# An attention and gated feed-forward kernel on one core: the second unit's softmax sums inverted on GpSimd, the third unit's outputs as three accumulating products, and an earlier copy of transposed scores

## The chip, the cores and the metric

The kernel runs on one core of one Trainium2 chip. A core has five engines that run their own instruction streams in order and meet through semaphores: TensorE (PE in the profile; its weight loads are listed as PEld), VectorE (DVE), ScalarE (ACT), GpSimd (POOL) and SyncE (SP), which here issues the DMAs. The metric is the device time of one execution in microseconds. Before the change it is 1147.95 us, the median of three runs (1147.83 to 1148.65).

## The reference

The reference has two parts. First comes masked attention over q, k, v of 8 batches, 8 heads, 576 positions and 64 values a head. The first four heads see the last 32 positions, the last four every fourth of the last 128:

```python
scores = scale * np.matmul(q, k.transpose(0, 1, 3, 2))
mask_plain = (rel >= 0) & (rel < window)
mask_dil = (rel >= 0) & (rel < window * dilation) & (rel % dilation == 0)
scores = np.where(masks[None, :, :, :], scores, -1000000000.0)
attn = np.exp(scores - np.max(scores, axis=-1, keepdims=True))
attn = attn / (np.sum(attn, axis=-1, keepdims=True) + 1e-09)
return np.matmul(attn, v)
```

The heads are put side by side, which makes x with 4608 rows of 512, and x goes through a normalised, gated feed-forward layer of width 1536:

```python
xn = x / np.sqrt(np.mean(x * x, axis=-1, keepdims=True) + 1e-06) * rms_g
g = xn @ w_gate
silu = g * (1.0 / (1.0 + np.exp(-g)))
return silu * (xn @ w_val) @ w_out
```

All values are float32. The weights arrive as 64-bit floating-point words and are turned into 32-bit ones on the chip.

## The kernel before

**Units and bursts.** The 4608 rows are cut into 16 units of 288 (half a batch each). The attention of a unit is cut into 14 bursts: a pair of heads with 96 queries (three bursts for each of the first two pairs) or 72 queries (four for each of the last two). A burst goes through these stages: the scores on TensorE (`scored`, L486 or L489), their maximum on DVE (`scores_max`, L361 and L366), the exponentials on ACT, which also add up the sums (`scores_exp`, L376), the inversion of the sum and the scaling by it (`scores_norm`, L384 to L393), the transposition on TensorE (`transposed`, L463), its copy out of PSUM (`untranspose`, L446 and L448), the product with v (`output`, L472, or L477 and L478), and the copy of the outputs into x (`take`, L408 or L411, and for some units `add`, L421).

**Exact and split units.** The first two units (`u < NNAT`, NNAT is 2) multiply plain float32 numbers. From the third on, every operand is split into a rounded high part and a low part in float32r, and a product is made of three: high by high, high by low, low by high. For the outputs of these units the kernel makes one wide product of v's high part with both parts of the scores (L477: 4 times the queries as columns) and one of v's low part (L478: 2 times), the latter added in PSUM to the first half of the former. The two halves are then added in SBUF: `take` copies the second half (ACT, L411), `add` adds the first half from PSUM (DVE, L421).

**The scaling of a burst.** For the first unit it stands on DVE mostly, for the second on ACT (L389), from the third on, on POOL (L391). The sum and its inverse are made on DVE for all of them (L385 and L386; before that, in the first unit, L384).

**The feed-forward layer.** A unit's layer is 12 rounds of three program steps: `gate` (the gate's products of one block of 128 columns; part 0), `val` (the value's products; part 1), and `proj` (the output products of the block before; part 2). The gate's and the value's products go to two PSUM banks in turn: the gate of the next block takes the bank of this block's value. A bank is free when the value product on DVE (`prod`, L679) has read it and, where a transposition was written into the rest of the same bank, when that has been copied out too. Outputs of attention have one bank, scores one.

**Order.** Nothing is reordered: the program's order is each engine's order. One number, `now`, counts the program steps; `later(dt, rank, fn)` puts work off to the start of a later step, and `flush` emits it there by rank, ahead of the products of that step. A burst's scores are made in some step; the maximum follows one step later, the exponentials two (rank 2), for the second unit the inversion and the scaling three (rank 2.1). Transpositions follow after 5 steps, the second unit's outputs after 7 and the third unit's after 8. The attention of a unit lies beside the feed-forward layer of the unit before it.

**What else lies beside the second unit's attention.** While the first unit's layer runs (about 41 to 129 us), the weights are still being decoded. A piece is loaded by DMA, rebased (`rebase`: ACT L159 makes a scaled copy, then POOL L162 scales the piece in place), and put together by two operations on DVE in two successive steps (`rest`, L177, and `whole`, L181). The rebasing of the next piece is emitted at the end of the step in which `rest` was emitted (rank 8.9). In every second step a weight is also split for the later units (rank 6: ACT L242 and then DVE or POOL L243).

**Other lines named below.** `gate` puts a tanh on ACT (L661) and a product on DVE (L666); `square` (ACT L427, then L433 on POOL or DVE) sums the squares for the normalisation; `rms_root` (L536 to L543) takes the root on POOL; `split_v` makes the parts of v (ACT L301, POOL L305); `split` those of q and k (L330 to L344); `parts` those of the hidden values (ACT L690, POOL L691).

Of the kernel before, what the change touches and what calls it, by code (L numbers as in the profile page):

```python
# [9 lines left out]
F32 = mybir.dt.float32  # L10
# [4 lines left out]
ALU = mybir.AluOpType  # L15
# [10 lines left out]
QB = 96  # L26
NC = DM // P
NJ = FF // P
NNAT = 2
# [23 lines left out]
def geometry(u, c):  # L53


    half = u % 2
    if c < NC // 2:
        if half:
            return [(QB * i, QB * i, 0, P) for i in range(U // QB)], QB, U + W
        return [(QB * i, max(QB * i - W, 0), 0 if i else W, P if i else QB)  # L60
                for i in range(U // QB)], QB, U
    nq = U // DIL
    keys = nq + (W if half else 0)
    return [(nq * r, keys * r, 0 if half else W, keys) for r in range(DIL)], nq, keys * DIL
# [3 lines left out]
def attn_moe(ctx: ExitStack, tc: tile.TileContext, qk_in, v_in, w_gate, w_val, w_out, rms_g, outT):  # L68
# [4 lines left out]
    V, A, G, PE = nc.vector, nc.scalar, nc.gpsimd, nc.tensor  # L73

    cst = ctx.enter_context(tc.tile_pool(name="cst", bufs=1))
# [11 lines left out]
    G.memset(inv, 1.0 / DM)  # L87
    mhalf = cst.tile([QB, U // QB], F32, name="mhalf")
    G.memset(mhalf, -0.5)
    mask = cst.tile([QB, P], F32, name="mask")  # L90
    G.memset(mask, 0.0)
    G.affine_select(out=mask, in_=mask, pattern=[[-1, P]], compare_op=ALU.is_ge,
# [14 lines left out]
    now = [0]  # L107
    put_off = {}

    def later(dt, rank, fn):  # L110
        put_off.setdefault(now[0] + dt, []).append((rank, fn))
# [173 lines left out]
    def further(b, n):  # L285

        k = everything.index(b) + n
        return everything[k] if k < len(everything) else None
# [90 lines left out]
    def scores_norm(u, c, i):  # L379
        blocks, nq, _ = geometry(u, c)  # L380
        n = blocks[i][3]
        t, sm = st[u, c, i]
        if u == 0:
            V.tensor_reduce(out=sm[:nq, :, 1], in_=t[:nq, :, :n], axis=mybir.AxisListType.X, op=ALU.add)  # L384
        V.tensor_reduce(out=sm[:nq, :, 3], in_=sm[:nq, :, 1:3], axis=mybir.AxisListType.X, op=ALU.add)  # L385
        V.reciprocal(out=sm[:nq, :, 3], in_=sm[:nq, :, 3])  # L386
        for a in range(2):
            if u == 1:
                A.activation(out=t[:nq, a, :n], in_=t[:nq, a, :n], func=AF.Copy, scale=sm[:nq, a, 3:4])  # L389
                continue  # L390
            (V if u == 0 and (c, i) > (NC - 1, 0) else G).tensor_scalar(  # L391
                out=t[:nq, a, :n], in0=t[:nq, a, :n], scalar1=sm[:nq, a, 3:4],
                scalar2=1.0, op0=ALU.mult, op1=ALU.mult)  # L393

    def take(u, c, i, o):

        blocks, nq, _ = geometry(u, c)
        if (u, c) not in xraw:
            xraw[u, c] = sb.tile([P, U], F32, tag="xraw", name=f"xraw_{u}_{c}", bufs=NC)
        x = xraw[u, c]  # L400
        if c < NC // 2:
            to = x[:, QB * i:QB * i + nq]
        else:
            to = x.rearrange("p (j r) -> p r j", r=DIL)[:, i, :]
        copy = V.tensor_copy if i % 2 and u == 0 and c == NC - 1 else A.copy
        if u < NNAT:
            for a in range(2):
                copy(out=to[a * D:(a + 1) * D], in_=o[a * D:(a + 1) * D, a * nq:(a + 1) * nq])  # L408
        else:
            for a in range(2):  # L410
                A.copy(out=to[a * D:(a + 1) * D], in_=o[a * D:(a + 1) * D, (2 + a) * nq:(3 + a) * nq])  # L411
        if i == len(blocks) - 1:
            later(1, 2.5 if u else 1.9, lambda: square(u, c))
# [9 lines left out]
    def square(u, c):  # L423
        first = c == 0
        sq = sb.tile([P, U], F32, tag="xsq" if first else "tmp", name=f"sq_{u}_{c}", bufs=1 if first else 2)
        x = xraw[u, c]
        A.activation(out=sq, in_=x, func=AF.Square)  # L427
        if u == 0:
            G.tensor_scalar(out=x, in0=x, scalar1=gs[:, c:c + 1], scalar2=1.0, op0=ALU.mult, op1=ALU.mult)
        if first:  # L430
            xsq[u] = sq
        else:
            later(1, 0.4, lambda: (V if c == NC - 1 else G).tensor_tensor(out=xsq[u], in0=xsq[u], in1=sq, op=ALU.add))  # L433
# [6 lines left out]
    def untranspose(b, t_ps):  # L440
        blocks, nq, _ = geometry(*b[:2])
        n = blocks[b[2]][3]
        t_in = t_ps[:n].rearrange("k (a q) -> k a q", a=2)[:, :, :nq]
        exact = b[0] < NNAT
        st[b] = pt = sb.tile([P, 2, 2, QB], F32 if exact else F32R, tag="pt", name=f"pt_{b[0]}_{b[1]}_{b[2]}", bufs=2)
        A.copy(out=pt[:n, 0, :, :nq], in_=t_in)  # L446
        if not exact:
            V.tensor_tensor(out=pt[:n, 1, :, :nq], in0=t_in, in1=pt[:n, 0, :, :nq], op=ALU.subtract)  # L448

    def products(q, t, o, t_ps, s_tag="s", o_tag="o"):  # L450


        if q:
            s_ps = ps.tile([P, 512], F32, tag=s_tag, name=f"s_{q[0]}_{q[1]}_{q[2]}")
        if o:
            o_ps = ps.tile([P, 512], F32, tag=o_tag, name=f"o_{o[0]}_{o[1]}_{o[2]}")
            pt = st.pop(o)
        if t:
            p, _ = st.pop(t)
        def transposed(a):  # L460
            blocks, nq, _ = geometry(*t[:2])
            n = blocks[t[2]][3]
            PE.transpose(t_ps[:n, a * QB:a * QB + nq], p[:nq, a, :n], ident[:nq, :nq])  # L463

        def output(a):
            blocks, nq, _ = geometry(*o[:2])
            n = blocks[o[2]][3]
            if a:
                return
            out = o_ps[:, :2 * nq].rearrange("d (a q) -> d a q", a=2)  # L470
            if o[0] < NNAT:
                PE.matmul(out, vs.pop(o)[:n].rearrange("k a d -> k (a d)"), pt[:n, 0, :, :nq], start=True, stop=True)  # L472
                return
            vh, vl = (part[:n].rearrange("k a d -> k (a d)") for part in vparts[everything.index(o) % 2])

            both = o_ps[:, :4 * nq].rearrange("d (t a q) -> d t a q", t=2, a=2)
            PE.matmul(both, vh, pt[:n, :, :, :nq], start=True, stop=False)  # L477
            PE.matmul(out, vl, pt[:n, 0, :, :nq], start=False, stop=True)  # L478

        def scored(a):  # L480
            blocks, nq, _ = geometry(*q[:2])
            qc, kc, _, n = blocks[q[2]]
            sv = s_ps[:QB].rearrange("q (a t k) -> q a t k", a=2, t=2)
            if q[0] < NNAT:
                qk = heads[q[0], 2 * q[1] + a]
                PE.matmul(sv[:nq, a, 0, :n], qk[:, qc:qc + nq], qk[:, U + kc:U + kc + n], start=True, stop=True)  # L486
                return
            qs, ks = heads[q[0], 2 * q[1] + a]
            PE.matmul(sv[:nq, a, :, :n], qs[:, qc:qc + nq], ks[:, :, kc:kc + n], start=True, stop=True)  # L489

        parts = [(b, fn, a) for b, fn in ((t, transposed), (o, output), (q, scored)) for a in range(2)]
        for b, fn, a in parts:
            if b:
                fn(a)
        if t:
            later(1, 0.2, lambda: untranspose(t, t_ps))
        if o:
            later(1, 0.5, lambda: take(*o, o_ps))
            if o[0] >= NNAT:
                later(1, 4, lambda: add(*o, o_ps))  # L500
            if o[0] < NNAT:
                later(1, 9, lambda: load_v(further(o, 3)))
            far = further(o, 2)
            if far and far[0] >= NNAT:
                split_v(far, 11 if o[0] < NNAT else 1)
        if q:
            later(1, 0.7, lambda: scores_max(*q, s_ps))
            later(2, 2, lambda: scores_exp(*q))
            later(3 if q[0] < NNAT else 4, 2.1 if q[0] == 1 else -1, lambda: scores_norm(*q))
            u, c, i = q  # L510
            nxt = after(u, 2 * c, 2)
            nb = len(geometry(u, c)[0])
            if u < NNAT:
                if u == NNAT - 1 and c == NC - 1 and i == nb - 1:
                    for a in range(2):
                        later(1, 9, lambda a=a: load(NNAT, a))
                        later(5 + a, 9, lambda a=a: split(NNAT, a, (1, 2, 2, 3), G, V))
            elif nxt and i == 0:
                split(*nxt, (1, 2, 2, 3), G, V)
                split(nxt[0], nxt[1] + 1, (2, 3, 3, 4), G, V)  # L520
# [240 lines left out]
    ends = nb + LAG + OUT + 5  # L761
# [8 lines left out]
    for n in range(ends):  # L770
# [4 lines left out]
        t_ps = None  # L775
        if "t" in events.get(n, {}):
            t_ps = ps.tile([P, 512], F32, tag="gv"[n % 2] if n < nb + LAG else "acc0", name=f"t_first_{n}")[:, :2 * QB]
# [12 lines left out]
    for u in range(NU):  # L790
        for j in range(NJ):
            for part in range(0 if u + j else 2, 3):
                t = 3 * (u * NJ + j) + part
# [92 lines left out]
```

## Time and profile before

| what | value |
|---|---|
| median of three runs | 1147.95 us (1147.83 to 1148.65) |
| the profiled execution | 1148.22 us |
| its span | 1146.4 us |
| granted TensorE clock, mean | 0.997 |
| PE, busy | 1120.8 us (98%) |
| DVE, busy | 793.4 us (69%) |
| ACT, busy | 714.6 us (62%) |
| POOL, busy | 620.8 us (54%) |
| chain that ended last | PE 85%, DVE 6%, ACT 4%, issue 2%, DMA 1%, POOL 1% |

A row of the timeline gives the start and the time taken in us, the engine, the line of the kernel, the operation, what is written and read, and its shape; in brackets stands how long the engine had been idle before it, and what ended that. A row of the waits gives the engine and line that waited, the one it waited for, the us in total, how often, and the longest. The busy time of TensorE is no measure of its full speed, since successive products overlap; a gap between them is lost time all the same.

### The profile page before, as it was taken

What the parts mean: (1) busy time and instruction counts of PE and PEld (TensorE: products, weight loads), DVE (VectorE), ACT (ScalarE), POOL (GpSimd) and SP (SyncE); (2) the same over time, 40 slices, a digit from 0 to 9 for tenths busy, and PEclk for the clock granted to TensorE, in tenths of its full rate; (3) what the DMA queues carried; (4) which work ended last, traced back from release to release, by engine and by line L of the source; (5) the groups of instructions that cost most, each with busy time, mean ns of one, the idle gap of its engine ahead of it and who ended that gap; (6) DMA issues with size and microseconds to landing.
All of it is one profiled execution on the core that took longest, in us unless ns stands there. A gap on an engine that the chain in (4) does not pass through costs nothing.

```text
span 1146.4 us, 25956 instructions
## 1 busy us (share of the span) xinstructions
PE 1120.8 (98%) x8357; PEld 1088.0 (95%) x8357; DVE 793.4 (69%) x2893; ACT 714.6 (62%) x2610; POOL 620.8 (54%) x1073
## 2 busy tenths in 40 slices
PE   8898888999999999999999999999999999999998
PEld 7676778999999999999999999999999999999998
DVE  7889865867767586776758677585866758586411
ACT  5686676766657576675757657576765757576311
POOL 8235576655546465564547556465655646565211
PEclk9999999999999999999999999999999999999999
DMA  9555211311212121121212213121221312120000
GB/s 246 168 202 205 89 48 38 93 50 50 83 38 82 40 84 52 52 89 33 79 41 83 58 41 94 34 86 41 71 63 45 95 27 87 41 79 15 2 21 21
DMA packets 61545, 82.19 MB, mean 72 GB/s; under 512 B 7298, under 2 KB 41090, under 8 KB 61410
## 3 DMA queue, kind: packets, MB, share of 16 engines
q1 hardware_dynamic: 61410, 80.54, 23.6%
q8 instruction: 67, 1.10, 0.4%
q14 instruction: 68, 0.56, 0.2%
HBM read 71.08 MB, written 9.44 MB: 70 GB/s over the span
## 4 chain that ended last, share of the span: by engine, by line
PE 85%; DVE 6%; ACT 4%; issue 2%; DMA 1%; POOL 1%; POOLq 0%; SPq 0%; DVEq 0%; ACTq 0%
PE acc L622 8%; PE g L622 8%; PE v L622 8%; PE acc L623 8%; PE g L624 8%; PE g L623 8%; PE acc L624 8%; PE v L623 8%; PE v L624 8%; PE s L489 3%; PE o L477 3%; PE o L478 1%; PE busy L739 1%; ACT t L376 1%; DVE lo L243 1%
## 5 line engine op out<-in xcount | busy, mean ns | idle before, releaser
L691 POOL TENSOR_TENSOR hlo<-th,hhi 128x288 fp32r<-128x288 f32 x180 | 145.2, 807 | 201.5 <-ACT hhi L690 153.7
L624 PE MATMUL acc<-hhi,lo 128*128 128x288 f32 x720 | 212.2, 295 | 0.0
L391 POOL TENSOR_SCALAR t<-t,sum 72x72 f32<-72x72 f32 (+3 forms) x414 | 154.0, 384 | 71.9 <-DVE sum L386 65.2
L624 PE MATMUL v<-xhi,lo 128*128 128x288 f32 x612 | 180.8, 295 | 0.0
L624 PE MATMUL g<-xhi,lo 128*128 128x288 f32 x612 | 180.6, 295 | 0.0
L376 ACT ACTIVATE t<-t,sum 96x128 f32<-96x128 f32 (+3 forms) x448 | 165.6, 375 | 11.7 <-DVE sum L366 11.0
L690 ACT CAST hhi<-th 128x288 fp32r<-128x288 f32 x180 | 78.1, 434 | 141.0 <-DVE th L679 138.8
L305 POOL TENSOR_TENSOR vlo<-vt,vhi 128x128 fp32r<-128x128 f32 x196 | 93.3, 476 | 109.3 <-ACT vhi L301 96.9
L421 DVE TENSOR_TENSOR xraw<-o,xraw 64x96 f32<-64x96 f32 (+1 forms) x392 | 106.8, 272 | 56.4 <-ACT xraw L411 50.4
L661 ACT ACTIVATE th<-g 128x288 f32<-128x288 f32 x180 | 73.9, 410 | 106.6 <-PE g L624 87.7
L624 PEld LDWEIGHTS acc<-hhi,lo 128*128 128x128 f32 x720 | 135.6, 188 | 0.0
L666 DVE SCALAR_TENSOR_TENSOR th<-th,g 128x288 f32<-128x288 f32 x180 | 80.4, 447 | 69.4 <-ACT th L661 69.4
L624 PEld LDWEIGHTS v<-xhi,lo 128*128 128x128 f32 x612 | 115.3, 188 | 0.0
L624 PEld LDWEIGHTS g<-xhi,lo 128*128 128x128 f32 x612 | 115.0, 188 | 0.0
L622 PE MATMUL g<-xhi,hi_g 128*128 128x288 f32 x357 | 110.7, 310 | 1.6 <-DVE sum L385 0.9
L335 POOL TENSOR_TENSOR ks<-qk,ks 128x288 fp32r<-128x288 f32 (+2 forms) x112 | 111.0, 1005 | 0.0
L622 PE MATMUL acc<-hhi,hi_o 128*128 128x288 f32 x360 | 110.8, 308 | 0.0
L411 ACT COPY xraw<-o 64x96 f32<-64x96 f32 (+1 forms) x392 | 101.5, 259 | 12.5 <-PE o L478 10.1
L679 DVE TENSOR_TENSOR th<-th,v 128x288 f32<-128x288 f32 x180 | 81.5, 453 | 38.1 <-PE v L624 30.0
L623 PE MATMUL acc<-hlo,hi_o 128*128 128x288 f32 x360 | 106.9, 297 | 0.0
L361 DVE TENSOR_TENSOR t<-s,mask 96x256 f32<-96x256 f32 (+3 forms) x196 | 71.5, 365 | 50.9 <-PE s L489 45.7
L623 PE MATMUL g<-xlo,hi_g 128*128 128x288 f32 x322 | 94.8, 294 | 0.0
(184 smaller groups left out, 3581.2 us busy)
## 6 DMA issues: line engine op xcount, KB each, us to landing
qk<-in_qk_dram SPq DMA_DIRECT2D x60, 288.0 KB, 2.8
vt<-in_v_dram SPq DMA_DIRECT2D x196, 64.0 KB, 1.9
qk<-in_qk_dram SPq DMA_DIRECT2D x30, 352.0 KB, 3.0
out_dram<-ot SPq DMA_DIRECT2D x64, 144.0 KB, 1.9
qk<-in_qk_dram SPq DMA_DIRECT2D x30, 304.0 KB, 2.8
raw<-in_w_gate_dram SPq DMA_DIRECT2D x12, 512.0 KB, 4.7
raw<-in_w_val_dram SPq DMA_DIRECT2D x12, 512.0 KB, 5.3
raw<-in_w_out_dram SPq DMA_DIRECT2D x12, 512.0 KB, 4.3
```

Source lines behind the costliest of these rows:

```text
L305: G.tensor_tensor(out=vl, in0=vs.pop(b), in1=vh, op=ALU.subtract)
L335: ek.tensor_tensor(out=ks[:, 1, :nkt], in0=kr, in1=ks[:, 0, :nkt], op=ALU.subtract)
L376: A.activation(out=t[:nq, a, :n], in_=t[:nq, a, :n], func=AF.Exp, scale=-1.0, bias=sm[:nq, a, 0:1], accum_out=sm[:nq, a, 1:2] if u else None)
L391: (V if u == 0 and (c, i) > (NC - 1, 0) else G).tensor_scalar(out=t[:nq, a, :n], in0=t[:nq, a, :n], scalar1=sm[:nq, a, 3:4], scalar2=1.0, ...
L411: A.copy(out=to[a * D:(a + 1) * D], in_=o[a * D:(a + 1) * D, (2 + a) * nq:(3 + a) * nq])
L421: V.tensor_tensor(out=to[rows], in0=o[rows, a * nq:(a + 1) * nq], in1=to[rows], op=ALU.add)
L622: PE.matmul(out, wh[:, cc, :], xh, start=start, stop=False)
L623: PE.matmul(out, wh[:, cc, :], xl, start=False, stop=False)
L624: PE.matmul(out, wl[:, cc, :], xh, start=False, stop=stop)
L666: V.scalar_tensor_tensor(out=t, in0=t, scalar=1.0, in1=g, op0=ALU.add, op1=ALU.mult)
L679: V.tensor_tensor(out=t, in0=t, in1=v_ps[:, :U], op=ALU.mult)
L691: G.tensor_tensor(out=lo, in0=t, in1=hi, op=ALU.subtract)
```

## The change

It has three parts. In the second unit (u = 1), the sum and its inverse are made on POOL, with an addition and a power of -1, in place of a reduction and a reciprocal on DVE; a small tile of -1 is set at the start. In the third unit (u = 2), the outputs are three products that accumulate in the same PSUM columns; `take` copies that half directly, and the later `add` falls away; the units after it stay as they were. And where a transposition was written into a value's bank (part 1 of a round), its copy is emitted ahead of the value product (rank -0.1 in place of 0.2; the value product has rank 0).

```diff
@@ -87,6 +87,8 @@
     mhalf = cst.tile([QB, U // QB], F32, name="mhalf")
     G.memset(mhalf, -0.5)
+    minus = cst.tile([QB, 2], F32, name="minus")
+    G.memset(minus, -1.0)
@@ -382,8 +384,12 @@
         t, sm = st[u, c, i]
         if u == 0:
             V.tensor_reduce(out=sm[:nq, :, 1], in_=t[:nq, :, :n], axis=mybir.AxisListType.X, op=ALU.add)
-        V.tensor_reduce(out=sm[:nq, :, 3], in_=sm[:nq, :, 1:3], axis=mybir.AxisListType.X, op=ALU.add)
-        V.reciprocal(out=sm[:nq, :, 3], in_=sm[:nq, :, 3])
+        if u == 1:
+            G.tensor_tensor(out=sm[:nq, :, 3], in0=sm[:nq, :, 1], in1=sm[:nq, :, 2], op=ALU.add)
+            G.tensor_tensor(out=sm[:nq, :, 3], in0=sm[:nq, :, 3], in1=minus[:nq], op=ALU.pow)
+        else:
+            V.tensor_reduce(out=sm[:nq, :, 3], in_=sm[:nq, :, 1:3], axis=mybir.AxisListType.X, op=ALU.add)
+            V.reciprocal(out=sm[:nq, :, 3], in_=sm[:nq, :, 3])
@@ -403,7 +409,7 @@
-        if u < NNAT:
+        if u <= NNAT:
             for a in range(2):
                 copy(out=to[a * D:(a + 1) * D], in_=o[a * D:(a + 1) * D, a * nq:(a + 1) * nq])
         else:
@@ -472,6 +478,10 @@
             vh, vl = (part[:n].rearrange("k a d -> k (a d)") for part in vparts[everything.index(o) % 2])
+            if o[0] == NNAT:
+                for k, (vp, t) in enumerate(((vh, 0), (vh, 1), (vl, 0))):
+                    PE.matmul(out, vp, pt[:n, t, :, :nq], start=k == 0, stop=k == 2)
+                return
@@ -493,10 +503,10 @@
         if t:
-            later(1, 0.2, lambda: untranspose(t, t_ps))
+            later(1, -0.1 if now[0] >= ends and (now[0] - ends) % 3 == 2 else 0.2, lambda: untranspose(t, t_ps))
         if o:
             later(1, 0.5, lambda: take(*o, o_ps))
-            if o[0] >= NNAT:
+            if o[0] > NNAT:
                 later(1, 4, lambda: add(*o, o_ps))
```

## The prediction

> **What bounds the kernel now.** First the busy times by stretch (TensorE alone, then one stretch with all engines; the columns are the length, then busy us and count per engine), because the share over the whole span mixes stages.
>
> ```profile
> 44.00:92.00 48.00, 44.06 (x219) 0.96 0.58 209
> 200.00:1146.00 946.00, 942.18 (x7329) 1.00 0.19 57
> 60.00:80.00 20.00, 20.00 (x108) 16.30 (x107) 16.75 (x44) 18.15 (x58) 7.83 (x6) 1.00 0.55 195
> ```
>
> From 200 us on TensorE stands still for 946 - 942.18 = 3.8 us in all, and the change leaves the number of columns that it streams there as it is: nothing is to be won there. What the change can move lies before 200 us. Between 60 and 80 us TensorE is full, but ACT is at 18.15 of 20 and DVE at 16.75: ACT has almost no air, and it runs in order, so a new wait on ACT stays on ACT. POOL is at 7.83 and looks free; what matters is what stands ahead in its queue, not its load.
>
> Next, who held TensorE up between 130 and 200 us, where the third unit's attention runs:
>
> ```profile
> PE v L622 <- DVE pt L448: 3.3, 2, 1.8
> PE s L489 <- DVE sum L366: 1.7, 2, 1.0
> PE o L477 <- DVE xraw L421: 1.6, 2, 0.9
> ```
>
> DVE is the last to end in all three: here taking work off DVE pays, and at most some 10 us (these and five smaller rows of that answer).
>
> **Part 1: the second unit's inversion on POOL.** What goes is small: a sum and a reciprocal on DVE for each of 14 bursts.
>
> ```profile
> 59.49 0.15 DVE L385 TENSOR_REDUCE sum<-sum 72x2 f32<-72x4 f32 x1
> 59.67 0.16 DVE L386 RECIPROCAL sum<-sum 72x2 f32<-72x2 f32 x1
> 59.76 1.20 DVE L181 SCALAR_TENSOR_TENSOR f<-f,raw 128x1024 uint32<-128x1024 uint32 x1
> ```
>
> 14 x 0.31 = 4.3 us of DVE. What comes is an add and a power on POOL. The trace has no such pair on two columns; the nearest are the root's operations on three columns, free and beside DVE's decoding:
>
> ```profile
> 198.70 0.86 POOL L537 TENSOR_TENSOR rst<-rst,mhalf 96x3 f32<-96x3 f32 x1 [3.70 <-DVE rst L536]
> 199.89 0.46 POOL L543 TENSOR_TENSOR rst_lo<-rst,rst_hi 96x3 fp32r<-96x3 f32 x1
> 111.71 1.85 POOL L537 TENSOR_TENSOR rst<-rst,mhalf 96x3 f32<-96x3 f32 x1
> ```
>
> So the pair takes 0.46 + 0.86 and a hand-over, 1.4 us, and 2.4 us where the power is held up as at 111.71. I take 1.4 to 2.0, nearer the free rows, since two columns are less than three. The Trainium skill (SBUF — State Buffer, section Who interferes with whom) says that a DVE instruction with two SBUF inputs and a GpSimd one share a port pair, and that whichever starts first holds it for its whole length. The rows of L537 (0.86 and 1.85) agree; by that rule each of the pair could wait out a 1.2 us decoding operation, an estimate of up to 3.8 us for both, and part 1 would come out at its high end below, 10.5.
>
> The price is not the pair but its place. The inversion's result is waited for by ACT's scaling (L389) in the same step. In every second step a weight piece was rebased at the step's end: ACT L159, then POOL L162, which waits for L159. The inversion of the following step stands behind that L162. Five of the fourteen bursts fall so. DVE could do its two operations at once; POOL can't.
>
> *Place 1, at 60 us.* ACT, then POOL, from narrow windows of the timeline (start, us, and in brackets the idle time before):
>
> ```profile
> 58.63 1.14 ACT L159 ACTIVATE f<-raw 128x1024 f32<-128x1024 f32 x1
> 59.79 0.32 ACT L446 COPY pt<-v 128x192 f32<-128x192 f32 x1
> 60.01 0.65 ACT L389 ACTIVATE t<-t,sum 72x104 f32<-72x104 f32 x2
> 61.41 0.47 ACT L408 COPY xraw<-o 64x96 f32<-64x96 f32 x2
> 62.66 1.16 ACT L159 ACTIVATE f<-raw 128x1024 f32<-128x1024 f32 x1
> 65.64 0.64 ACT L389 ACTIVATE t<-t,sum 72x104 f32<-72x104 f32 x2
> 59.85 2.12 POOL L162 TENSOR_SCALAR raw<-raw 128x1024 f32<-128x1024 f32 x1 [4.12 <-DVE sum L386]
> 63.96 1.12 POOL L162 TENSOR_SCALAR raw<-raw 128x1024 f32<-128x1024 f32 x1 [2.00 <-ACT f L159]
> ```
>
> L162 starts at 59.85 and takes 1.12 when free, 2.12 beside DVE's L181: it ends between 61.0 and 62.0. With the pair, L389 starts between 62.4 and 64.0 instead of 60.01; I take 63.1, so ACT is 3.1 late. Behind L389 stand the squares, the weight split, and the copies of the last outputs (L408, ended 61.88). There is one bank for outputs, so TensorE's next outputs wait for these copies. TensorE's places, here and below:
>
> ```profile
> 63.68 0.52 PE L472 MATMUL o<-pt,v 128*128 128x192 f32 x2
> 68.74 0.34 PE L486 MATMUL s<-qk 128*72 128x104 f32 x2
> 78.57 0.46 PE L472 MATMUL o<-pt,v 104*128 104x144 f32 x2
> 84.17 0.51 PE L619 MATMUL g<-xn,f 128*128 128x288 f32 x1 [0.50 <-ACT pt L446]
> ```
>
> 61.88 + 3.1 = 65.0 against 63.68: TensorE 1.3 late (0.5 to 2.2).
>
> *Place 2, at 65.64.* ACT carries its 3.1 along. L159 now ends at 63.82 + 3.1 = 66.9, L162 at 68.05, the pair at 69.5 to 70.1; I take 70.0. ACT itself would be there at 65.64 + 3.1 = 68.7, so 1.3 comes on top: 4.4 late. Behind L389 come the weight split's copy, DVE's half of the split, the value product and the scores' maximum, which frees the one bank of scores:
>
> ```profile
> 68.16 0.08 DVE L366 DVE_READ_ACCUMULATOR2_ANT sum<- 72x1 f32 x1
> ```
>
> It ended at 68.24, TensorE's scores came at 68.74: 0.5 of air, TensorE 3.9 late (2.4 to 4.6).
>
> *Places 3 and 4, at 76 and 82.*
>
> ```profile
> 74.76 1.15 ACT L159 ACTIVATE f<-raw 128x1024 f32<-128x1024 f32 x1
> 76.11 0.65 ACT L389 ACTIVATE t<-t,sum 72x104 f32<-72x104 f32 x2
> 77.18 0.58 ACT L408 COPY xraw<-o 64x72 f32<-64x72 f32 x2
> 78.53 1.19 ACT L159 ACTIVATE f<-raw 128x1024 f32<-128x1024 f32 x1
> 81.57 0.64 ACT L389 ACTIVATE t<-t,sum 72x104 f32<-72x104 f32 x2
> 77.66 1.22 POOL L433 TENSOR_TENSOR sq<-sq,sq 128x288 f32<-128x288 f32 x1
> ```
>
> ACT has some air in between and comes to place 3 about 3.1 late, paced by TensorE (3.9 less 0.8, the air at 78.57 counted below). L159 ends at 75.91 + 3.1 = 79.0, L162 at 80.15; the sum of squares (L433) stands ahead of the inversion too: 81.4; the pair ends at 82.8 to 83.4, I take 83.1. ACT is 7.0 late. The copies that ended at 77.76 end at 84.8 and the outputs of 78.57 wait: TensorE 6.2 late. Place 4: L159 ends at 79.72 + 7.0 = 86.7, L162 at 87.85, the pair at 89.3 to 89.9, I take 89.8; ACT alone would come at 88.6: 1.2 more, 8.2 late. That reaches the gate products of 84.17 through the split and the value product. They also waited 0.50 for the copy at that place, which part 3 puts ahead: some 0.35 comes back, TensorE 7.9 late. The two steps after give back about 0.5 (waits of that size on ACT, which is then less late than TensorE). A fifth place, near 49 us, costs 0 to 1.3, since ACT comes there early; I take 0.3. The sum is 7.9 - 0.5 + 0.3 = 7.7, with 4.5 at every low end and 10.5 at every high end. From 92 to 130 us DVE's decoding runs in the same order behind the same late steps; I see nothing in it that makes the time good.
>
> **Part 2: the third unit's outputs.** 28 additions leave DVE:
>
> ```profile
> 130.00:200.00 70.00, 7.61 (x28) 0.98 0.19 54
> ```
>
> That is DVE's time at L421 alone. It counts only where DVE ends a wait: the output bank is free after ACT's copies (the 1.6 us above go), and two additions, 0.54, come out of the chain ahead of four waits of scores and gates. Not all of it stays, for ACT's chain (output copies, exponentials, splits) is next late at three of these places. I take 2.5 in all together with part 3, between 0.5 (the bank alone, and another wait taking most of it) and 6.0 (over half of the 10 us).
>
> On TensorE, one product of 288 columns and one of 144 become three of 144:
>
> ```profile
> 178.67 0.37 PE L477 MATMUL o<-pt,vhi 72*128 72x288 f32 x1 [0.91 <-DVE xraw L421]
> 178.88 0.23 PE L478 MATMUL o<-pt,vlo 72*128 72x144 f32 x1
> 178.95 0.34 PE L622 MATMUL v<-xhi,hi_o 128*128 128x288 f32 x1
> ```
>
> From start to start 0.21 and 0.07, 0.28 in all; three of 0.07 are 0.21. The number of columns is the same, so I take 0 for the 14 bursts, with -1.0 (14 x 0.07) and +0.7 as the ends, since one more weight load could show. The Trainium skill (TensorE: Matmul & The Clock Gate, section Back-to-back issue gap) gives about 81 ns for 128 columns; with that, an estimate, three would take 0.24 and the sum would move by less than 0.6 over all bursts.
>
> **Part 3: the copy first in a value's bank.**
>
> ```profile
> ACT pt L446 <- DVE th L679: 101.2, 70, 2.5
> ```
>
> ACT's copy waited 70 times for the value product, which reads the same bank; the order is now turned round, and the product waits for the copy. Where DVE is last, ACT's copy and the hand-over, some 0.4 us, leave the chain to the next gate products (in part 2's 2.5). Where ACT is last, DVE stands behind it: at 59.79 the copy came right after L159, and the product, with DVE's decoding behind it, now waits for it. That costs nothing extra while ACT holds DVE at L243 anyway. From 200 us on there is room in both orders; I take 0, up to +1.
>
> **The sum.** The profiled execution took 1148.22 us (span 1146.4); 1148.22 + 7.7 - 2.5 = 1153.4. It lies 0.3 above the median of the runs, 1147.95; so 1153.1. Ends: +4.5 - 6.0 = -1.5 gives 1146.5; +10.5 - 0.5 + 1 = 11 gives 1159.0.
>
> **Rivals.**
> *POOL is in time.* If POOL ran the inversion ahead (the exponentials' sums are there a step earlier), ACT would lose nothing and even save its waits for the reciprocal, and parts 2 and 3 would remain: 1148 - 2.5 - 0.5 = 1145. For it: nine of fourteen inversions have a free POOL ahead of them. Against it: the five rows of L162 and L389; an in-order queue can't pass L162. It decides at the air of 1.8 us at 63.68. 0.15.
> *It cancels.* The low end of part 1 against the high end of part 2: 1147 to 1149. 0.10.
> *The shared port makes it worse.* Each of the pair is held up by DVE's decoding in all bursts, by 1 us or more: part 1 reaches 10 or over, 1157 to 1160. For it: 111.71. Against it: at the five places DVE mostly waits for ACT just then. 0.12.
> *The product behind the copy becomes a bound* after 200 us, where ACT is inside another operation: TensorE's 3.8 us of standing still would double, with part 1 as forecast 1157. 0.05.
> My forecast: 0.58.
>
> **Chances.** About 0.2%, 2.3 us, is what a measurement can tell from no change. Slower by more: 0.58 + 0.12 + 0.05 = 0.75; within: 0.10; faster: 0.15. The range 1146.5 to 1159.0 leaves out most of the first rival and the upper part of the third, under 0.2.
>
> **What would show it.** Right: ACT waits for POOL at L389 near 60, 66, 76 and 82 us, 8 us or more in all; outputs on TensorE wait for L408 near 64 and 80; 92 us of before comes near 99. L421 is gone, TensorE's waits between the third unit's bursts shrink by 2 to 3 us. Wrong: L389 starting without a wait, or TensorE as full between 55 and 83 us as before; or the third unit's stretch shorter by 5 us or more.

## The result and the profile after

The changed kernel takes 1162.51 us, the median of four runs (1161.36 to 1162.87), against 1147.89 us for the kernel before beside it: a ratio of 1.0126 [1.0108, 1.0143]. It is slower by 14.6 us, on the side that the prediction took and 9.4 us beyond its value, outside its range. The profiled execution took 1162.32 us, its span is 1160.2 us.

In the new file lines have moved: the rebasing is L161 and L164, the inversion L388 and L389, ACT's scaling L395, the output copies L414 and L417, the additions L427, the copies of transposed scores L452 and L454, the second unit's outputs L478, the value product L689, the rounding of the hidden values L700.

TensorE by stretch (length, busy us and count, clock, DMA share, GB/s):

```profile
44.00:92.00 48.00, 39.00 (x180) 0.89 0.43 152
92.00:130.00 38.00, 33.72 (x144) 0.96 0.58 202
130.00:200.00 70.00, 61.12 (x414) 0.98 0.19 57
200.00:1160.00 960.00, 952.95 (x7407) 1.00 0.19 56
```

Between 44 and 92 us TensorE issues 180 products in place of 219, stands still for 9.0 us in place of 3.9, and its granted clock has gone from 0.96 to 0.89. After 200 us it stands still for 7.05 us in place of 3.8. Following one and the same product through both traces gives the delay directly: 10.8 us at 130 us, some 9.9 at 200, 13.8 at the end. So the loss has three parts: +10.8 where the second unit's attention lies, -0.9 where the third's lies, and +3.9 over the rest.

**The first stretch.** ACT's largest row of waits between 30 and 105 us, and the five scalings that waited longest (in brackets the idle time and what ended it):

```profile
ACT t L395 <- POOL sum L389: 12.9, 7, 3.6
```

```profile
49.80 0.69 ACT L395 ACTIVATE t<-t,sum 96x128 f32<-96x128 f32 x2 [2.27 <-POOL sum L389]
64.58 0.65 ACT L395 ACTIVATE t<-t,sum 72x104 f32<-72x104 f32 x2 [2.85 <-POOL sum L389]
71.55 0.38 ACT L395 ACTIVATE t<-t,sum 72x104 f32<-72x104 f32 x1 [1.28 <-POOL sum L389]
86.19 0.65 ACT L395 ACTIVATE t<-t,sum 72x104 f32<-72x104 f32 x2 [3.62 <-POOL sum L389]
92.92 0.38 ACT L395 ACTIVATE t<-t,sum 72x104 f32<-72x104 f32 x1 [1.21 <-POOL sum L389]
```

What stood ahead of the second and the fourth in POOL's queue:

```profile
61.47 1.14 POOL L164 TENSOR_SCALAR raw<-raw 128x1024 f32<-128x1024 f32 x1 [4.61 <-ACT f L161]
62.55 1.21 POOL L388 TENSOR_TENSOR sum<-sum 72x2 f32<-72x2 f32 x1
63.85 0.70 POOL L389 TENSOR_TENSOR sum<-sum,minus 72x2 f32<-72x2 f32 x1
...
82.36 1.13 POOL L164 TENSOR_SCALAR raw<-raw 128x1024 f32<-128x1024 f32 x1 [3.83 <-ACT f L161]
83.43 1.79 POOL L439 TENSOR_TENSOR sq<-sq,sq 128x288 f32<-128x288 f32 x1
85.18 0.19 POOL L388 TENSOR_TENSOR sum<-sum 72x2 f32<-72x2 f32 x1
85.45 0.70 POOL L389 TENSOR_TENSOR sum<-sum,minus 72x2 f32<-72x2 f32 x1
```

POOL stood idle for 4.61 and 3.83 us ahead of L164, which waited for ACT; then came L164, once the sum of squares, and only then the pair. These are the five places and the order that the prediction named. From its start to its end the pair takes 1.0 us where nothing holds it up, as at 85.18, and 2.0 where the addition is held up, as at 62.55.

TensorE's standstills that followed, and its clock in three windows of the length in which that changes:

```profile
52.56 0.97 PE L496 MATMUL s<-qk 128*72 128x104 f32 x4 [3.98 <-DVE sum L368]
74.22 0.40 PE L496 MATMUL s<-qk 128*72 128x104 f32 x2 [2.41 <-DVE sum L368]
87.87 0.51 PE L478 MATMUL o<-pt,v 104*128 104x144 f32 x2 [1.73 <-ACT xraw L414]
95.23 0.51 PE L629 MATMUL g<-xn,f 128*128 128x288 f32 x1 [2.20 <-DVE h L689]
```

```profile
51.40:58.23 6.83, 5.67 (x17) 0.50 0.44 149
75.30:78.71 3.41, 3.41 (x12) 0.50 0.20 49
95.80:99.21 3.41, 3.41 (x10) 0.50 0.57 205
```

The clock is exactly halved, for 3.41 us or twice that. The first stretch begins within the standstill of 3.98 us, the other two 1.1 and 0.5 us behind those of 2.41 and 2.20 us; a fourth comes at 181.1 us. The kernel before has one such stretch in these places and one later:

```profile
52.30:55.71 3.41, 3.41 (x10) 0.50 0.48 196
147.90:151.31 3.41, 3.41 (x18) 0.50 0.02 5
```

Up to 130 us, half of TensorE's busy time at half clock is lost: (5.67 + 3.41 + 3.41) / 2 = 6.2 us after, 3.41 / 2 = 1.7 before, so, as an estimate, up to 4.5 us of the 10.8 is clock and not waiting. The Trainium skill (TensorE: Matmul & The Clock Gate, section What's actually happening) tells of a free-running window of 3413 ns and a gate that passes either all pulses or half of them, with half after an idle window; the stretches agree in length and in depth, but the standstill of 2.20 us ahead of 95.8 us is shorter than such a window.

**The later stretches.** Who held TensorE up between 130 and 205 us, the rows that answer to those of before:

```profile
PE v L632 <- DVE pt L454: 3.3, 3, 1.6
PE g L629 <- DVE h L689: 1.1, 1, 1.1
```

The wait of the outputs for the additions (1.6 us) is gone; that of the scores for the maxima (1.7) is down to 0.2. From 205 us on these rows lead; the kernel before has the second with 0.4 us and nothing like the first:

```profile
PE o L487 <- DVE xraw L427: 2.2, 6, 0.4
PE o L487 <- ACT pt L452: 1.0, 1, 1.0
```

### The profile page after: what moved, and what is told of

It reads as the page before. It is cut to its first block, busy times and chain, and to the rows that moved or that the text cites. A ratio compares the mean times of both kernels' runs of the same rounds, so it can differ in the third digit from the quotient of the medians.

```text
span 1160.2 us, 25893 instructions
## 1 busy us (share of the span) xinstructions
PE 1127.4 (97%) x8371; PEld 1092.4 (94%) x8371; DVE 783.1 (67%) x2837; ACT 720.8 (62%) x2610; POOL 640.2 (55%) x1102
## 4 chain that ended last, share of the span: by engine, by line
PE 81%; DVE 6%; ACT 6%; POOL 3%; issue 2%; DMA 1%; POOLq 0%; SPq 0%; DVEq 0%; ACTq 0%
PE acc L632 8%; PE v L632 8%; PE g L632 8%; PE acc L633 7%; PE v L633 7%; PE v L634 7%; PE g L634 7%; PE g L633 7%; PE acc L634 7%; PE s L499 3%; PE o L487 2%; PE busy L749 1%; DVE qs L346 1%; PE o L488 1%; PE g L629 1%
## 5 line engine op out<-in xcount | busy, mean ns | idle before, releaser
L700 ACT CAST hhi<-th 128x288 fp32r<-128x288 f32 x180 | 77.9, 433 | 202.3 <-DVE th L689 197.7
L427 DVE TENSOR_TENSOR xraw<-o,xraw 64x72 f32<-64x72 f32 (+1 forms) x364 | 99.2, 273 | 53.0 <-ACT xraw L417 48.4
L689 DVE TENSOR_TENSOR th<-th,v 128x288 f32<-128x288 f32 x180 | 81.0, 450 | 32.3 <-PE v L634 31.0
L346 DVE TENSOR_TENSOR qs<-qk,qs 64x288 fp32r<-64x288 f32 x112 | 91.3, 816 | 11.0 <-ACT qs L341 7.9
L417 ACT COPY xraw<-o 64x72 f32<-64x72 f32 (+1 forms) x364 | 93.8, 258 | 7.2 <-PE o L488 5.1
```

Source lines behind the costliest of these rows:

```text
L346: eq.tensor_tensor(out=qs[D:], in0=qr[D:], in1=qs[D:], op=ALU.subtract)
L427: V.tensor_tensor(out=to[rows], in0=o[rows, a * nq:(a + 1) * nq], in1=to[rows], op=ALU.add)
L689: V.tensor_tensor(out=t, in0=t, in1=v_ps[:, :U], op=ALU.mult)
```

## The experiments

The medians, with the kernel before in the same comparison. The first four kernels ran on one chip, the next four on a second and the last three on a third, so kernels of different groups are compared by their ratios.

| kernel | what it has | median us | before us | ratio |
|---|---|---|---|---|
| p1_only | part 1 | 1158.68 | 1148.71 | 1.0086 [1.0069, 1.0103] |
| p2_only | part 2 | 1146.25 | 1148.71 | 0.9973 [0.9962, 0.9984] |
| p3_only | part 3 | 1154.99 | 1148.71 | 1.0055 [1.0040, 1.0070] |
| p1_nine | part 1 for nine bursts | 1145.40 | 1148.71 | 0.9973 [0.9962, 0.9985] |
| p1_early | part 1, issued a step earlier | 1145.56 | 1148.26 | 0.9976 [0.9966, 0.9986] |
| p1_fill | part 1, TensorE kept busy | 1154.63 | 1148.26 | 1.0052 [1.0037, 1.0067] |
| p3_skip | part 3 without three copies | 1149.60 | 1148.26 | 1.0014 [1.0004, 1.0024] |
| nine_p2 | p1_nine and part 2 | 1143.03 | 1148.26 | 0.9951 [0.9936, 0.9966] |
| before_fill | before, TensorE kept busy | 1148.25 | 1148.67 | 0.9997 [0.9988, 1.0007] |
| p2_p3 | parts 2 and 3 | 1152.25 | 1148.67 | 1.0033 [1.0024, 1.0043] |
| early_p2 | p1_early and part 2 | 1143.18 | 1148.67 | 0.9948 [0.9934, 0.9963] |

**Each part alone.** Each kernel takes its part's lines of the change's diff and no others.

Part 1:

> The inversion on GpSimd alone. If the place in GpSimd's queue is what costs (five inversions behind a rebase): TensorE stands still about 6 to 7 us more than before between 44 and 100 us, with the half-speed stretches that follow about 10 us in all, so 1156 to 1160. If the loss of the full change came from its parts together (the value product behind the copy): under 1153.

Part 2:

> The three products without the later additions, alone. My forecast said about 2 us faster: 1145.5 to 1147. The rival, that another wait takes the place of the removed one: within 0.5 us of before.

Part 3:

> The copy first, alone. If it is this part that costs some 0.35 us in every second unit after 200 us (the outputs wait for the later addition): 2 to 4 us slower from 200 us on, 1149.5 to 1152 in all. If the 4 us lost there in the full change were late transfers by chance: 1147 to 1149.

Part 1 costs 10.0 us, part 2 brings 2.5, part 3 costs 6.3, which is above both of its expected ranges: they had left out that it costs early as well. The sum, 13.8, is within a microsecond of the whole change's 14.6, but in part by chance. By stretch the parts don't add: at 130 us the delays of parts 1 and 3, 10.2 and 3.0, would make 13.2 where the changed kernel is 10.8 late, and between 130 and 200 us it wins 0.9 where part 2 alone wins 2.0. Part 1's delay stands at 10.2 us at 130 us and moves little afterwards (10.85 at the end). Part 2's gain falls where it was looked for, 2.0 us of it between 130 and 200 us. The kernel before has a halved stretch at 147.9 us and part 2 alone has none there, but that isn't the gain: p1_only and before_fill have none there either, and against the kernel before they stand at 200 us where they stood at 140, within 0.1 us. Part 3's cost, which the prediction put at 0 to 1, has two halves: 3.0 us up to 130 us and 3.5 after 200.

**Is it the place in POOL's queue, or the pair itself?** Two kernels change the place and leave the pair's operations as they are. In p1_nine the five bursts whose scaling waited behind a rebasing keep their inversion on DVE:

```diff
-        if u == 1:
+        if u == 1 and now[0] - ends + 2 not in (4, 8, 10, 14, 16):
             G.tensor_tensor(out=sm[:nq, :, 3], in0=sm[:nq, :, 1], in1=sm[:nq, :, 2], op=ALU.add)
```

> The inversion on GpSimd alone, but the five bursts whose inversion stands behind a rebase keep it on VectorE. By place: nothing is lost, 1147 to 1149. By the price of the operations on GpSimd: nine fourteenths of the loss of the first kernel, about 6 us, so 1153 to 1155.

In p1_early all fourteen are on POOL, issued at the end of `scores_exp`, one step earlier and so ahead of the rebasing:

```diff
     def scores_exp(u, c, i):
...
+        if u == 1:
+            G.tensor_tensor(out=sm[:nq, :, 3], in0=sm[:nq, :, 1], in1=sm[:nq, :, 2], op=ALU.add)
+            G.tensor_tensor(out=sm[:nq, :, 3], in0=sm[:nq, :, 3], in1=minus[:nq], op=ALU.pow)
...
     def scores_norm(u, c, i):
...
-        if u == 1:
-            G.tensor_tensor(out=sm[:nq, :, 3], in0=sm[:nq, :, 1], in1=sm[:nq, :, 2], op=ALU.add)
-            G.tensor_tensor(out=sm[:nq, :, 3], in0=sm[:nq, :, 3], in1=minus[:nq], op=ALU.pow)
-        else:
+        if u != 1:
```

> All fourteen inversions on GpSimd, but issued one step earlier, behind the exponentials and ahead of the rebase. If the place in the queue is the whole cost: no wait of the scaling for GpSimd over 0.6 us, and 1144.5 to 1147, as with nine on GpSimd. If GpSimd's slower operations or the shared port cost by themselves: 1150 or more.

Both turn a loss of 10.0 us into a gain, 3.3 and 2.7; for p1_nine 1147 to 1149 us had been the better of the two expectations. TensorE between 44 and 100 us, in part 1 alone, then in p1_nine, then in p1_early:

```profile
44.00:100.00 56.00, 44.97 (x201) 0.88 0.48 170
```

```profile
44.00:100.00 56.00, 53.42 (x266) 1.00 0.63 223
```

```profile
44.00:100.00 56.00, 53.08 (x264) 1.00 0.61 222
```

And POOL in p1_early at the place that waited 2.85 us in the changed kernel:

```profile
60.16 0.96 POOL L381 TENSOR_TENSOR sum<-sum 72x2 f32<-72x2 f32 x1 [1.33 <-ACT t L378]
61.19 0.70 POOL L382 TENSOR_TENSOR sum<-sum,minus 72x2 f32<-72x2 f32 x1
61.88 1.13 POOL L164 TENSOR_SCALAR raw<-raw 128x1024 f32<-128x1024 f32 x1
```

The pair now runs as soon as the exponentials' sums are there, in the time that POOL used to spend waiting, and L164 follows it. The addition is held up here too (0.96 against 0.19 free), with no harm. So the place costs, not the pair: the rival that the shared port decides falls, since p1_early has all fourteen pairs and gains. The expectation that no scaling waits over 0.6 us for POOL was missed by one wait of 1.10 us at 36 us, ahead of all these rebasings; the changed kernel and p1_nine have it too.

Most of the gain arises at one place, TensorE's standstill near 50 us, first in the kernel before and then in p1_nine:

```profile
51.85 0.58 PE L486 MATMUL s<-qk 128*72 128x104 f32 x4 [2.83 <-DVE sum L366]
```

```profile
50.25 0.58 PE L492 MATMUL s<-qk 128*72 128x104 f32 x4 [1.79 <-DVE sum L368]
```

The wait for the maximum is 1.0 us shorter, and no half clock follows it. Ahead of the kernel before by 0.6 us at 48 us, p1_nine is ahead by 1.6 at 52 and by 3.3 at 56 us. That DVE has less work there is the likely reason; no run tests it alone.

**How much of part 1 is TensorE's clock?** In p1_fill products whose result nobody reads are issued ahead of the waiting ones, into a bank that is free at that time; everything else is part 1 alone:

```diff
+    def fill(n, tag):
+        f = ps.tile([P, 512], F32, tag=tag, name=f"fill_{now[0]}")
+        for _ in range(n):
+            PE.matmul(f, ones, ones[:, None, :].to_broadcast([P, 4, P]), start=True, stop=True)
+
+    FILLS = {(5, "scored"): (14, "v"), (11, "scored"): (8, "v"), (15, "output"): (5, "g"), (18, "gate"): (8, "v")}
```

> The inversion on GpSimd alone, and useless products in the four places where TensorE stood still for it (near 50, 72, 86 and 93 us), into a bank that is free then, so that its clock has no reason to fall. If the half-speed stretches after the standstills cost time of their own: the granted clock stays 1.0 from 44 to 100 us and 1153 to 1156 (3 to 5 us less than without). If other engines bind there anyway: 1157 to 1160.

```profile
44.00:100.00 56.00, 52.08 (x257) 1.00 0.50 181
```

The clock is full in all of the stretch, and the delay at 130 us falls from 10.2 to 6.0 us. The medians differ by 4.05 us, and by 3.6 when each is taken against its own kernel before. ACT still waits for POOL at L395, 11.7 us against 12.1. So about 4 us of part 1 is the halved clock behind its waits.

The same was tried on the kernel before, whose clock is halved once at 52.3 us:

```diff
+    FILLS = {(5, "scored"): (11, "v")}
```

> The kernel before, with eleven useless products (some 2.3 us) where TensorE stands still for 2.8 us near 49 us. If the half-speed stretch that follows that standstill costs 1.7 us by itself: 1146 to 1147, with the clock at 1.0 from 44 to 92 us. If others bind there: 1148 as before.

Here it brought nothing clear of noise: 0.9997 [0.9988, 1.0007], with a full clock throughout. TensorE was 1.66 us ahead from 56 to 66 us, 0.6 from 84 to 110 us and 1.2 at 130 us. Between 44 and 100 us its two largest waits were then these:

```profile
PE g L622 <- ACT pt L446: 1.0, 2, 0.6
PE s L486 <- DVE sum L366: 0.8, 2, 0.5
```

ACT and DVE don't follow the faster TensorE there, and part of the lead is given back as waits. That I expected a gain was wrong: a stretch at half clock costs its whole time only where TensorE is the last to end afterwards too.

The two kernels with useless products both have a full clock, so together they show what part 1's waits cost alone: at 130 us p1_fill is 7.2 us behind before_fill, having been 0.6 ahead at 48 us. Against the kernel before it is only 6.0 behind, because that one has a halved stretch.

**What does the copy first cost, and where?** The early half. ACT and then DVE in p3_only near 77 us:

```profile
76.44 1.12 ACT L159 ACTIVATE f<-raw 128x1024 f32<-128x1024 f32 x1
77.59 0.28 ACT L446 COPY pt<-v 104x144 f32<-104x144 f32 x1
79.09 0.65 ACT L389 ACTIVATE t<-t,sum 72x104 f32<-72x104 f32 x2 [1.22 <-DVE sum L386]
```

```profile
77.90 0.45 DVE L679 TENSOR_TENSOR h<-h,v 128x288 f32<-128x288 f32 x1 [1.66 <-ACT pt L446]
...
78.64 0.15 DVE L385 TENSOR_REDUCE sum<-sum 72x2 f32<-72x4 f32 x1
78.83 0.17 DVE L386 RECIPROCAL sum<-sum 72x2 f32<-72x2 f32 x1
```

DVE's product waits 1.66 us for a copy that stands behind the rebasing on ACT; behind the product stand the maximum, the sum and the reciprocal; and for the reciprocal ACT waits 1.22 us. The wait comes back to the engine that caused it. In p3_skip the three transpositions of such steps keep the old order:

```diff
-            later(1, -0.1 if now[0] >= ends and (now[0] - ends) % 3 == 2 else 0.2, ...)
+            later(1, -0.1 if now[0] >= ends and (now[0] - ends) % 3 == 2
+                  and now[0] - ends + 2 not in (7, 13, 19) else 0.2, ...)
```

> The copy first alone, but not for the three transpositions of the second unit whose copy stands behind a rebase on ACT. If the loss before 130 us comes from the value product waiting behind that: the lead of before comes back there (0 to 1 us late at 130 us), the loss of 3 to 4 us after 200 us stays, 1150.5 to 1153. If every copy first costs: 1154 to 1156 as with all.

The delay at 130 us goes from +3.0 to -0.6 us and the median from 1154.99 to 1149.60 (6.3 and 1.3 us above its own kernel before), just under the expected 1150.5 to 1153. Not all of it is the copies' doing: 1.2 of the 3.6 us are there at 58 us already, ahead of the first of the three copies, where the clock of p3_only was halved for 6.83 us and that of p3_skip for 3.41. The other 2.4 come later. The half after 200 us stays, 2.5 us, and so does its wait for the additions, which neither part 2 alone nor part 1 alone has:

```profile
PE o L477 <- DVE xraw L421: 1.7, 5, 0.4
```

How that arises is read from one value's bank, first in the kernel before, DVE's product with its half of the copy behind it (L448, the subtraction that makes the low part) and then ACT's two steps:

```profile
209.72 0.43 DVE L679 TENSOR_TENSOR th<-th,v 128x288 f32<-128x288 f32 x1
210.53 0.36 DVE L448 TENSOR_TENSOR pt<-v,pt 128x192 fp32r<-128x192 f32 x1 [0.39 <-ACT pt L446]
```

```profile
210.18 0.32 ACT L446 CAST pt<-v 128x192 fp32r<-128x192 f32 x1 [1.05 <-DVE th L679]
210.40 0.43 ACT L690 CAST hhi<-th 128x288 fp32r<-128x288 f32 x1
```

And in p3_only, ACT and then DVE, where this point of the program comes 3.06 us later:

```profile
212.67 0.32 ACT L446 CAST pt<-v 128x192 fp32r<-128x192 f32 x1 [0.50 <-PE v L463]
213.78 0.43 ACT L690 CAST hhi<-th 128x288 fp32r<-128x288 f32 x1 [0.78 <-DVE th L679]
```

```profile
213.02 0.36 DVE L448 TENSOR_TENSOR pt<-v,pt 128x192 fp32r<-128x192 f32 x1 [0.18 <-ACT pt L446]
213.30 0.44 DVE L679 TENSOR_TENSOR th<-th,v 128x288 f32<-128x288 f32 x1
```

The copy is earlier (212.67 - 3.06 = 209.61 in place of 210.18), the product later (210.24 in place of 209.72), and the hidden values are rounded 0.32 us later (210.72 in place of 210.40). From the third unit on a copied transposition has this second half on DVE, and the change puts it, too, ahead of the product. That is so in all 65 banks of a value after 205 us: against TensorE's own delay the product starts 0.4 us later in p3_only (the median of the 65) and 0.0 later in p1_nine, where the order is the old one. In the two traces the same delay of about a third of a microsecond then stands at what follows in both queues: ACT's next cast (L602), DVE's subtractions (L603, L344) and the addition L421, which frees the one bank of outputs. TensorE waits for it six times, up to 0.4 us each, 2.2 in all.

Whether the earlier copy helps the third unit:

> Parts two and three together, without the inversion on GpSimd. From the single parts: 3 us lost before 130 us, 2 us won from 130 to 200 us, 3 us lost after: 1151 to 1153. If the copy first takes half of what the removed additions give, as the full change looks between 130 and 200 us: only 1 us won there, and 1152 to 1154.

The median, 1152.25 us, lies in both ranges. With part 2 alone TensorE wins 2.0 us between 130 and 200 us; with parts 2 and 3 it wins 1.3. So the copy first adds nothing to the gain there. Whether it takes some of it isn't shown: a halved clock at 172.6 us, which part 2 alone doesn't have, can be up to 1.7 us of such a difference.

**The parts that pay, together.** With the inversion in its better places and without part 3:

> Nine inversions on GpSimd and the three products, without the copy first. If the gains add (3.3 and 2.5 us, in different stretches): 1142 to 1144. If one takes the other's (less air before 140 us makes the third unit's stretch tighter): 1144.5 to 1146.

> All inversions on GpSimd one step earlier, and the three products, without the copy first. If the gains add: 1142 to 1144, as with nine inversions there. If the shared port eats it: 1145 or more.

Both are faster than the kernel before by 0.5%: 1143.03 us (0.9951 [0.9936, 0.9966]) and 1143.18 us (0.9948 [0.9934, 0.9963]). They can't be told apart.

## Why the prediction was wrong, point by point

By the medians of the single parts, part 3 makes most of the 9.4 us that the result lies beyond the forecast: 6.3 us where the prediction had 0, up to 1. Part 1 adds 2.3 (10.0 for 7.7, still inside its 4.5 to 10.5), part 2 nothing, and 0.8 is left over.

**What bounds it.** Right as far as the runs show: none of the eleven kernels won more than some 0.5 us after 200 us, and a new wait on ACT between 60 and 80 us stayed.

**Part 1, the mechanism.** Right, and shown: the wait is POOL's queue order, at the five places named, and both kernels that change the place turn the loss into a gain. The sizes of the waits on ACT were near at the four places that were worked out: 3.1, 1.3, 3.9 and 1.2 us were expected, and 2.85, 1.28, 3.62 and 1.21 came. The pair was put at 1.4 to 2.0 us and takes 1.9 to 2.0 at four of the five places and 1.0 at the other.

**Part 1, its sum of 7.7.** The step that failed here is a term put at nothing: the sum took each wait once and left out TensorE's clock. Standstills of 2 to 4 us were followed by half clock, and that cost another 4 us (p1_fill). The waits alone are near the sum: 7.2 us at 130 us, p1_fill against before_fill. Place by place p1_fill falls behind by 1.2 us near 49 us, where 0.3 was taken, and by 1.3, 1.9, 1.8 and 1.9 at the four others, where 1.3, 2.6, 2.3 and 2.0 were; 0.5 comes back after that, as forecast. So the total is a little luckier than its terms. The hint at the clock was in the first row that it quoted, a granted clock of 0.96 between 44 and 92 us, and it made nothing of it. That from 92 to 130 us nothing makes the time good was nearly so: with part 1 alone the delay goes from 10.9 to 10.2 us there.

**Part 2 and the three products.** Right in size: part 2 alone brings 2.5 us (0.9973), so the three products cost nothing that shows. That part 3 would take part in it is not borne out: 1.3 us with it against 2.0 without, between 130 and 200 us.

**Part 3.** This is the other step that failed, and the larger one: "That costs nothing extra while ACT holds DVE at L243 anyway", and "From 200 us on there is room in both orders; I take 0, up to +1". Alone it costs 6.3 us. The first sentence followed DVE only up to L243. It left out that the maximum, the sum and the reciprocal stand behind the product too, and that ACT's next scaling waits for them. The second took the change for one copy on ACT against one product on DVE. It left out DVE's subtraction L448, which goes ahead of the product together with the copy, and the additions behind the product, for which TensorE's outputs wait. The rows of one bank and the starts in 65 show this; no run moves L448 alone. TensorE's standing still from 200 us on went from 3.8 us to 7.05: that is the size of the rival "the product behind the copy becomes a bound", to which 0.05 was given, though by another way than it named, and it came in addition to the forecast.

In the changed kernel part 3's early cost adds little to part 1's: the delay at 130 us is 10.8 us against 10.2 for part 1 alone. That the two waits lie on the same engines at the same steps, so that one covers the other, is the likely reason; no run tests it alone.

**The rivals.** "POOL is in time" was the wrong account of this change, but p1_early shows its premise: issued one step earlier, POOL is in time, and with part 2 the kernel takes 1143.2 us where that rival gave 1145. "It cancels" fell with parts 1 and 3. "The shared port makes it worse" came nearest in time (1157 to 1160) and was wrong in its cause. What stood against it was wrong too: at four of the five places the addition took 1.16 to 1.21 us, beside DVE's decoding. That is part of the wait there, and it costs nothing where POOL would have been idle.

## What to carry to other kernels

When small work moves to an idle engine, read what stands ahead of it in that engine's queue and what that waits for; then issue it where its operands are ready, not where its result is wanted. When two engines read one bank, the order of the reads decides which queue is held up: follow what stands behind the reader that now comes second until the wait reaches TensorE or dies. And look at the granted clock behind a standstill of TensorE of 2 us or more: here half clock cost another 4 us where TensorE ended last afterwards, and nothing clear of noise where it didn't.

## What was not expected of the hardware

The clock falls to exactly 0.50 for 3.41 us or twice that, and standstills shorter than that are enough: 2.20 us ahead of 95.8 us, 2.41 ahead of 75.3. Not each of them does it. The changed kernel's wait of 1.73 us at 87.87 has no halved stretch behind it, and neither has a standstill of 2.82 us near 50 us in p2_p3. Within a trace the stretches start whole multiples of 3.413 us apart (52.32 and 147.89 in the kernel before: 28 of them). Count off such intervals between 44 and 1130 us in the eight traces that have a stretch, and take those at full clock. Each one in which TensorE stood still for 2.1 us or more is followed by half clock, some with 1.4 to 1.8 us are, and none with less; p2_p3's 2.82 us fall on two intervals, 1.25 and 1.57. Where a standstill falls in the count differs from trace to trace, so there is luck in it. From kernel to kernel the stretch after 130 us comes at 146.9, 147.9, 166.3, 170.8, 172.6 or 181.1 us, or not at all. Half of 3.41 us, 1.7, is the most that one can cost.

The addition and the power of two columns on POOL, by line over the whole span (count, then shortest, median and longest in ns):

```profile
L388 POOL TENSOR_TENSOR sum<-sum x14: 188/674/1212, 35.3 to 97.6; 72x2 f32<-72x2 f32 x8, 96x2 f32<-96x2 f32 x6
L389 POOL TENSOR_TENSOR sum<-sum,minus x14: 688/698/1997, 35.6 to 98.9; 72x2 f32<-72x2 f32 x8, 96x2 f32<-96x2 f32 x6
```

So the addition takes 0.19 us free and up to 1.21, the power 0.69 and up to 2.00. The Trainium skill (SBUF — State Buffer, section Who interferes with whom) has it that a DVE instruction with two inputs from SBUF contends with a GpSimd one that reads SBUF, and that the lock on the shared ports is exclusive. The rows agree, the excess being about as long as a decoding operation on DVE (1.2 us).

One wait stays open. ACT's rounding of the hidden values (L700) waits for the transfer of outputs out of the buffer that it writes, and from 205 us on this adds up to more in every kernel with part 3:

```profile
ACT hhi L700 <- DMA out_dram<-ot: 3.4, 2, 2.2
```

That is 2.4 to 5.1 us with part 3, 0.5 to 1.8 without it. In the changed kernel the wait of 2.20 us at 840.78 us is followed by TensorE's one wait of 0.97 us for the copy. Why the transfer ends late there was not tried.
